# A fused attention and softplus layer on one core: a first product on 256 tokens, full-width transposes and a schedule planned around pieces of the instruction stream

## The chip, the cores and the metric

One core of a Trainium2 chip. The time is the device time of one execution in microseconds (us), and the median of several runs is quoted. Each experiment was timed in the same rounds as the kernel before, on the same chip, because chips differ: the kernel before had medians of 201.96 us in the first job and 198.81, 199.34, 199.85 and 199.41 us in the four later ones. So ratios are compared, not medians of different jobs. The profile comes from one extra execution of each kernel, and the span it covers is some 2 us shorter than the time.

## The reference, cut to what matters

```python
q, k, v, f_logit: (4, 8, 768, 48)          # batch, heads, tokens, head width
f = sigmoid(f_logit)
for t in range(768):                        # a gated running state for each head
    state = f[t][:, None] * state + outer(k[t], v[t])
    y[t] = q[t] @ state
x = y rearranged to (3072, 384)             # tokens, heads * width
out = softplus(x @ w_in) @ w_out            # w_in 384 x 2048, w_out 2048 x 384
```

The kernels cut the 3072 tokens into 24 blocks of 128. A block's attention is a chain of small matmuls; then come the "first product" (x @ w_in), the softplus, and the "second product" (@ w_out). TensorE does all matmuls. In these kernels every result goes to PSUM, which the program lays out as eight banks of 512 floats a partition, and ScalarE or VectorE reads ("evacuates") a bank before the program uses it again.

## The kernel before

The order of all instructions comes from a list scheduler that runs while the kernel is built. Each task has an engine, an estimated duration, what it depends on, and the PSUM banks that it takes (`acq`) and gives back (`rel`).

```python
    ps = [psum.tile([128, 512], FP32, name=f"ps{i}") for i in range(8)]   # one tile, one bank
    def bank(key):
        return ps[P.bank[key]]
    ...                                             # 32 small transposes a block
    def t_T(n):
        for x in range(2):
            for p in range(4):
                for u in range(2):
                    for g in range(2):
                        mm(o[g*64:g*64+64, c:c+64], a[u*64:u*64+64, x*8+g*4+p, :], ident[...],
                           is_transpose=True, tile_position=(u*64, g*64))
    ...
    def t_M(n, g):                                  # one evacuation for each bank
        ... in0=bank(("PU", n, g))[:, 0:256] ...
    def t_F1(n, b):                                 # 128 tokens: 12 matmuls of 128 columns to a bank
        for i in range(4):
            for j in range(3):
                mm(o[:, i*128:i*128+128], w_in[j][:, f*128:f*128+128], xT[n % NX][:, j, :], ...)
    ...                                             # transfers: 4 blocks, w_in, w_out, the rest
    for t in P.run():
        t.fn()
```

## Time and profile before

| | kernel before |
|---|---|
| time, first job | 201.96 us (199.61 to 203.14) |
| span in the profile | 198.9 us |
| TensorE busy | 174.9 us, 88% |
| VectorE, ScalarE busy | 93.3 us, 109.3 us |
| matmuls | 4184 |
| packets of TensorE's instruction stream | 32 |

The two products in the page's list of groups. The columns after the bar are busy time, mean ns of one, and the engine's idle time just before them with what ended most of it. PE is TensorE, PEld its weight loads, ACT ScalarE, DVE VectorE, POOL GpSimd and SP SyncE; "issue" means that nothing that the profile shows was waited for.

```profile
L187 PE MATMUL ps<-xT,w_in 128*128 128x128 bf16 x1152 | 78.1, 224 | 4.4 <-issue 1.6
...
L187 PE MATMUL ps<-w_out,G 128*128 128x384 bf16 x384 | 72.8, 326 | 0.0
```

### The profile page before, as it was taken

What the parts mean: (1) busy time and instruction counts of PE and PEld (TensorE: products, weight loads), DVE (VectorE), ACT (ScalarE), POOL (GpSimd) and SP (SyncE); (2) the same over time, 40 slices, a digit from 0 to 9 for tenths busy, and PEclk for the clock granted to TensorE, in tenths of its full rate; (3) what the DMA queues carried; (4) which work ended last, traced back from release to release, by engine and by line L of the source; (5) the groups of instructions that cost most, each with busy time, mean ns of one, the idle gap of its engine ahead of it and who ended that gap; (6) DMA issues with size and microseconds to landing.
All of it is one profiled execution on the core that took longest, in us unless ns stands there. A gap on an engine that the chain in (4) does not pass through costs nothing.

```text
span 198.9 us, 9400 instructions
## 1 busy us (share of the span) xinstructions
PE 174.9 (88%) x4184; PEld 136.9 (69%) x4184; DVE 93.3 (47%) x268; ACT 109.3 (55%) x241; POOL 54.9 (28%) x75
## 2 busy tenths in 40 slices
PE   0274689999988896999999989999999999999993
PEld 0153478877566675778777768786877778878861
DVE  4287941011774589364336234662455555551012
ACT  2464134559368675676787627864673455435420
POOL 6003860013562365153524012442244300000000
PEclk9999999999999999999999999999999999999999
DMA  6998999999878698899999898894011101110112
GB/s 127 186 204 159 137 200 205 182 197 186 173 148 170 136 181 194 168 197 199 188 188 214 165 210 191 185 229 152 10 36 43 43 3 43 43 46 3 40 40 79
DMA packets 106408, 27.34 MB, mean 137 GB/s; under 512 B 100480, under 2 KB 105600, under 8 KB 106368
## 3 DMA queue, kind: packets, MB, share of 16 engines
q1 hardware_dynamic: 103296, 23.60, 55.1%
q0 software_dynamic: 3072, 3.15, 10.4%
q8 instruction: 32, 0.52, 1.1%
q14 instruction: 8, 0.07, 0.1%
HBM read 25.17 MB, written 4.72 MB: 150 GB/s over the span
## 4 chain that ended last, share of the span: by engine, by line
PE 81%; SPq 6%; DMA 5%; issue 3%; DVE 2%; POOL 1%; DVEq 0%
PE ps L187 81%; SPq L221 6%; DMA w_in<-in_moe_w_in_dram 3%; DMA qkb<-in_k_dram 2%; POOL w_in L256 1%; DVE osb L442 1%; DVE st L361 1%; DVE xT L418 0%; DVE pm L342 0%; DVE tt L355 0%; DVE qkT L317 0%; DVEq L442 0%; DVEq L317 0%
## 5 line engine op out<-in xcount | busy, mean ns | idle before, releaser
L187 PE MATMUL ps<-xT,w_in 128*128 128x128 bf16 x1152 | 78.1, 224 | 4.4 <-issue 1.6
L432 ACT ACTIVATE G<-ps 128x512 bf16<-128x512 f32 x96 | 57.3, 597 | 40.3 <-PE ps L187 37.6
L187 PEld LDWEIGHTS <-w_in 128*128 128x128 bf16 x1152 | 70.0, 100 | 11.2 <-issue 3.9
L187 PE MATMUL ps<-w_out,G 128*128 128x384 bf16 x384 | 72.8, 326 | 0.0
L295 POOL TENSOR_TENSOR qs<-qkb,et 128x768 bf16<-128x768 f32 x20 | 33.0, 1652 | 72.9 <-issue 26.8
L187 PEld LDWEIGHTS <-G 128*128 128x128 bf16 x384 | 34.1, 98 | 17.3
L442 DVE COPY osb<-ps 128x384 f32<-128x384 f32 x24 | 13.3, 556 | 50.2 <-PE ps L187 48.8
L418 DVE COPY xT<-ps 128x192 bf16<-128x192 bf16 x48 | 10.2, 252 | 33.1 <-PE ps L187 25.2
L402 ACT ACTIVATE ysb<-ps 128x192 bf16<-128x192 f32 x48 | 13.5, 329 | 20.6 <-PE ps L187 19.6
L317 DVE COPY qkT<-ps 128x512 bf16<-128x512 bf16 x48 | 18.1, 416 | 7.5 <-PE ps L187 7.2
L342 DVE TENSOR_TENSOR pm<-ps,mask 128x256 bf16<-128x256 f32 x48 | 18.1, 416 | 4.5 <-PE ps L187 4.5
L282 ACT ACTIVATE et<-ps,bq 128x384 bf16<-128x384 f32 x24 | 13.9, 579 | 10.2 <-PE ps L187 10.1
L361 DVE SCALAR_TENSOR_TENSOR st<-tt,gt 128x192 bf16<-128x192 f32 x40 | 17.7, 442 | 1.0
L187 PEld LDWEIGHTS <-qs 64*64 64x64 bf16 x1120 | 15.0, 115 | 4.1 <-DVE qs L295 2.2
L187 PE MATMUL ps<-zt,negU 128*128 128x384 bf16 x24 | 8.5, 354 | 10.2 <-ACT zt L269 10.2
L269 ACT ACTIVATE zt<-fb 128x384 bf16<-128x384 f32 x24 | 12.6, 523 | 6.9 <-DMA fb<-in_f_logit_dram 6.9
L187 PEld LDWEIGHTS <-qkT 64*64 64x64 bf16 x736 | 11.3, 112 | 5.8 <-issue 2.2
L301 POOL CAST vs<-vb 128x384 bf16<-128x384 f32 x20 | 10.4, 524 | 15.5 <-DMA vb<-in_v_dram 15.3
L355 DVE SCALAR_TENSOR_TENSOR tt<-ps,st 128x192 f32<-128x192 f32 x40 | 14.1, 352 | 0.7
L286 ACT ACTIVATE et<-ps,bk 128x384 bf16<-128x384 f32 x24 | 13.8, 577 | 0.0
L187 PE MATMUL ps<-ident,qs 64*64 64x64 bf16 x768 | 11.4, 201 | 2.6 <-DVE qs L295 1.8
L187 PEld LDWEIGHTS <-zt 128*128 128x128 bf16 x96 | 6.2, 100 | 10.3 <-issue 8.5
(35 smaller groups left out, 88.8 us busy)
## 6 DMA issues: line engine op xcount, KB each, us to landing
fb<-in_f_logit_dram SPq DMA_DIRECT2D x24, 192.0 KB, 4.5
qkb<-in_k_dram SPq DMA_DIRECT2D x24, 192.0 KB, 4.2
qkb<-in_q_dram SPq DMA_DIRECT2D x24, 192.0 KB, 4.5
vb<-in_v_dram SPq DMA_DIRECT2D x24, 192.0 KB, 4.4
out_dram<-osb SPq DMA_DIRECT2D x24, 192.0 KB, 3.1
w_in<-in_moe_w_in_dram POOLq DMA_DIRECT2D x12, 128.0 KB, 5.3
w_out<-in_moe_w_out_dram POOLq DMA_DIRECT2D x4, 384.0 KB, 9.1
```

Of the source, the lines that this page charges most:

```text
L187: return pin(nc.tensor.matmul(out=out, lhsT=lhsT, rhs=rhs, start=start, stop=stop, skip_group_check=True, **kw))
L269: pin(nc.scalar.activation(out=zt[n % NZ].rearrange("t p g d -> t g p d")[:, :, :, 0:48], in_=fb[n % NL].rearrange("t (g p) d -> t g p d", ...
L282: pin(nc.scalar.activation(out=et[n % NE][:, 0], in_=bank(("A", n))[:, 0:384], func=AF.Softplus, bias=bq, scale=1.0))
L286: pin(nc.scalar.activation(out=et[n % NE][:, 1], in_=bank(("A", n))[:, 0:384], func=AF.Softplus, bias=bk, scale=-1.0))
L295: pin(eng.tensor_tensor(out=qs[n % NQS][:, :, 0:48], in0=qkb[n % NL].rearrange("t x h d -> t (x h) d"), in1=et[n % NE].rearrange("t x (h d ...
L317: pin(nc.vector.tensor_copy(out=qkT[n % NQT][:, u].rearrange("d x p t -> d (x p t)"), in_=bank(("TX", n, u)).bitcast(BF16)[:, 0:512]))
L342: pin(nc.vector.tensor_tensor(out=pm[n % NPM][:, g], in0=bank(("PU", n, g))[:, 0:256].rearrange("s (p t) -> s p t", p=4), in1=mask, op=ALU ...
L355: pin(nc.vector.scalar_tensor_tensor(out=tt[m % 2], in0=U, scalar=C_P, in1=st[m % NS], op0=ALU.mult, op1=ALU.add))
L361: pin(nc.vector.scalar_tensor_tensor(out=st[(m + 1) % NS], in0=tt[m % 2], scalar=C_UP, in1=gb, op0=ALU.mult, op1=ALU.mult))
L402: pin(nc.scalar.activation(out=ysb[n % NY][:, u], in_=bank(("Y", n, u))[:, 0:192], func=AF.Copy, bias=0.0, scale=1.0))
L432: pin(nc.scalar.activation(out=G[n % NGF][:, 4 * b:4 * b + 4, :].rearrange("f j t -> f (j t)"), in_=bank(("H", n, b)), func=AF.Softplus, b ...
L442: pin(nc.vector.tensor_copy(out=osb[n % NO], in_=bank(("O", n))[:, 0:DM]))
```

## The change

Its intent: fewer instructions for TensorE, so that the pieces of 16 KB (256 instructions) in which they arrive no longer stall it, and fewer, larger evacuations. The core of the diff:

```diff
+PAGE, PAGE0, FETCH = 256, 63, 4.8          # the scheduler now models the pieces
-    ps = [psum.tile([128, 512], FP32, name=f"ps{i}") for i in range(8)]
+    ps = [psum.tile([128, 2, 512], FP32, name=f"ps{i}") for i in range(4)]
     def bank(key):
-        return ps[P.bank[key]]
+        i = P.bank[key]
+        return ps[i // 2][:, i % 2]
+    def two(key):                           # both banks of a tile, for a joined evacuation
+        return ps[P.bank[key + (0,)] // 2]
     def t_T(n):                             # 8 transposes of 128 x 128 for 32 of 64 x 64
+                mm(o[:, i:i + 128], qs[n % NQS][:, x, p].rearrange("t g d -> t (g d)"), ident,
+                   is_transpose=True)
-    def t_M(n, g):                          # likewise the outputs (t_ye) and their transposes (t_xe)
+    def t_M(n):
+            ... in0=two(("P", n))[:, :, 0:256] ...
     def t_F1(n, b):                         # n now counts pairs of blocks
-                mm(o[:, i * 128:i * 128 + 128], ..., xT[n % NX][:, j, :], ...)
+                mm(bank(("H", n, b))[:, i * 256:i * 256 + 256], ..., xT[n % NX][:, j] (256 columns))
+    ORD = [2, 0, 4]                         # transfers: 2 blocks, w_in, 4 blocks, w_out, the rest
...                                          # cut: new scheduler rules, split of t_qs, buffer counts
```

## The prediction

> **What bounds the kernel now.** I read the page from the top, then the chain of waits, then the timeline of TensorE in two stretches. The page first:
>
> ```profile
> span 198.9 us, 9400 instructions
> PE 174.9 (88%) x4184; PEld 136.9 (69%) x4184; DVE 93.3 (47%) x268; ACT 109.3 (55%) x241; POOL 54.9 (28%) x75
> ...
> PE   0274689999988896999999989999999999999993
> ...
> q8 instruction: 32, 0.52, 1.1%
> ...
> PE 81%; SPq 6%; DMA 5%; issue 3%; DVE 2%; POOL 1%; DVEq 0%
> ```
>
> TensorE is the only engine near full, and it carries 81% of the chain that ended last. Its slices (5 us each) fill only from about 25 us; there are dips in slices 12 to 16 (55 to 80 us), then it is solid. VectorE (47%) and ScalarE (55%) have room. The queue of instructions brought 32 packets of 16 KB; 2 x 4184 records in 32 packets are 261 an instruction packet, so nearly all of these are TensorE's own stream. The chain in order of time says what the holes are:
>
> ```profile
> 13.59 4.21 DMA qkb<-in_k_dram
> ...
> 20.15 5.24 DMA w_in<-in_moe_w_in_dram
> 25.39 0.14 issue
> 25.52 2.88 PE ps L187 x34
> ...
> 63.27 0.78 issue
> ...
> 68.10 0.77 issue
> ...
> 76.89 1.64 issue
> ...
> 132.33 45.13 PE ps L187 x1145
> 177.51 17.98 PE ps L187 x232
> 195.56 0.56 DVE osb L442
> ```
>
> Two different things are seen. Up to 25.5 us the chain is transfers: w_in is queued behind the keys of block 3. Later there are pieces called "issue", where TensorE waits for no semaphore. I counted TensorE's records (loads and matmuls together, 63 taken as already passed at the start, as the new model assumes): the stalls before 64.05, 68.87, 78.53, 82.80 and 132.33 us all stand at the first record of a new group of 256, so they are waits for the instruction stream itself. Two neighbouring ones begin 4.82 us apart (64.05 and 68.87). Idle time of PE there: 0.78 + 0.77 + 1.64 + 0.16 = 3.35 us up to 83 us, and about 0.3 at 132, so some 4 us with the pipeline's refilling.
>
> Where TensorE is solid, the timeline prices each kind of work by the distance of starts (a row's own length holds the pipeline's latency too):
>
> ```profile
> 141.79 1.46 PE L187 MATMUL ps<-w_out,G 128*128 128x384 bf16 x8
> 143.18 0.31 PE L187 MATMUL ps<-vs,pm 64*64 64x48 bf16 x16
> 143.33 0.42 PE L187 MATMUL ps<-ident,qs 64*64 64x64 bf16 x32
> 143.58 0.30 PE L187 MATMUL ps<-qkT 64*64 64x64 bf16 x16
> 143.71 0.30 PE L187 MATMUL ps<-vs,qs 64*64 64x48 bf16 x16
> 143.84 0.33 PE L187 MATMUL ps<-st,qkT 64*64 64x48 bf16 x16
> 143.99 0.29 PE L187 MATMUL ps<-ident,ysb 64*64 64x64 bf16 x12
> 144.21 0.82 PE L187 MATMUL ps<-w_out,G 128*128 128x384 bf16 x4
> 144.93 1.51 PE L187 MATMUL ps<-xT,w_in 128*128 128x128 bf16 x24
> 146.28 0.33 PE L187 MATMUL ps<-zt,negU 128*128 128x384 bf16 x1
> 146.44 0.24 PE L187 MATMUL ps<-negsel,zt 128*128 128x2 bf16 x4
> 146.55 1.50 PE L187 MATMUL ps<-xT,w_in 128*128 128x128 bf16 x24
> ```
>
> First product: 24 matmuls from 144.93 to 146.28, 56 ns each. Second product: 0.82 us for 4 of which one lasts 0.326 (the page's mean), so (0.82 - 0.326) / 3 = 163 ns. Cumulative sums: 0.27 us. The merged section of a block's attention: 143.18 to 144.21, 1.03 us, of which the 32 small transposes are 0.25 (143.33 to 143.58); before it, 8 second-product matmuls took 1.39 us instead of 1.30, so entering the section costs 0.09 more. A block of 128 tokens: 48 x 0.056 = 2.70, 16 x 0.163 = 2.61, 0.27 and 1.12: 6.70 us. Times 24 blocks: 161 us. TensorE ends at 195.6, so about 35 us are lost: by 25.5 us about 21 (it has done the attention of less than four blocks, 4 to 5 us of work); then some 5 more up to 35 us, where first-product matmuls lie 106 ns apart ((2.51 - 0.29) / 21 in the stretch from 25.52); about 4 to the instruction stream; the last 5 to sections that are not merged before block 8 and short waits.
>
> **What the Trainium skill says.** "TensorE: Matmul & The Clock Gate", section "Back-to-back issue gap", gives N / 2.4 + 2.5 ns warm: 56, 109 and 162.5 ns at 128, 256 and 384 columns. The trace agrees at both widths that it has (56 and 163). Its Part 1 gives half the clock after idling, 107 ns at 128 columns; the trace has 106 before 35 us. Its Part 4, on transposes, measures about 275 ns for a full-width one in a kernel; the trace has only small ones, and I take the distance, not the duration, as for other matmuls. "Runtime: NRT & Kernel Launch", section "Instruction fetch mechanics", says that instructions come in 16 KiB blocks of 256 and that the crossing is "mostly hidden". The size agrees (261 records a packet); "mostly" does not hold between 60 and 83 us, where four crossings cost 3.35 us.
>
> **The change part by part.**
> 1. First product on 256 tokens: 1152 matmuls at 56 ns (64.5 us) become 576 at 109 (62.8): -1.7 us, and 1152 instructions fewer with the weight loads. Weight loads hide already (PEld 69%).
> 2. Full-width transposes: 768 small ones (24 x 0.25 = 6.0 us) become 192 of 128 columns: 8 x 56 = 0.45 a block, 10.8 us. That is +4.8 us of TensorE, with another 1152 instructions fewer. Parts 1 and 2 alone add 3 us: a block costs 6.83, all blocks 164 us.
> 3. Instructions: 4184 matmuls become 3032, so 2 x 3032 / 261 = 23 packets in place of 32. A block falls from 349 records to 253; at 6.8 us a block a packet is used up in 6.9 us, where it was 4.9, almost the 4.82 at which the crossings stalled. I expect 3 to 4 of the 4 us back.
> 4. Merged evacuations. A copy of 192 columns takes 252 ns and one of 512 takes 416: 0.51 ns a column and 153 fixed. Joining pairs saves about 0.15 x 3 kinds x 24 = 11 us of VectorE, and 24 x 0.17 = 4 us of ScalarE. Neither is on the path where TensorE is solid; it shortens the chains of the first blocks by perhaps 0.5 us each.
> 5. Order of transfers: two blocks, all of w_in, four blocks, w_out, the rest; before: four blocks, w_in, w_out, the rest. w_in can start when the queries of block 1 are in (about 11 us) rather than at 18.1, so its first half is there by 18 to 19 in place of 25.4. The first product starts at 20 when block 1's chain is through, not at 25.5. But blocks 2 to 5 then start at about 21, take 4.1 us each (16 issues took the sync queue to 17 us), and w_out is whole only at 46, where the second product began before 40. TensorE has gaps between 28 and 41 us in exchange. Work done by 46, by the prices above: attention of 5.5 blocks at 1.59 = 8.7, two pairs of first product 10.5, most of a pair of second 4.7: 24, so 22 us lost. Before, by 45: 4.5 x 1.39 + 3.5 x 2.70 + 1.6 x 2.61 = 20, so 25 lost. Gain 3 us.
> 6. Merging from block 6 rather than 8, and fewer split sections: perhaps 2 of the last 5 us.
>
> Sum: 164 of work + 22 up to 46 us + 4 later = 190 us for TensorE's end, against 195.6. With the same 3.3 us of last copy and store the span is 193, 5.6 us or 2.8% less. Compared with the median of 202.45 I take 196.
>
> **The rivals.** (a) The head gets worse: the second product waits for w_out and TensorE starves between 28 and 46 us, with the slow clock as well. The page speaks for it (the transfers already move 160 to 200 GB/s in this stretch and cannot be sped up), against it that three pairs of first product need no w_out. It would cost 3 to 6 us: 200 to 203. (b) Banks become the bound: first-product, second-product (two for a pair), transposes, scores and outputs ask for more than eight at times, so TensorE would wait for ScalarE's softplus (597 ns against 655 ns of matmuls a bank). Nothing is seen of that before (85 to 178 us is nearly solid); it would cost 0.1 to 0.3 us a block, 2 to 7 us: 198 to 203. (c) The head gains as much as w_in comes earlier, since TensorE later never catches up: 5 to 7 us rather than 3, and the time is 190 to 192. (d) Full-width transposes do not pipeline at 56 ns: at twice that +11 us, 206. The neighbouring full-width matmuls speak against it.
>
> **Range and chances.** The work (164) is known to 1 or 2 us, the head to about 4, the stalls to 2: together about 5, so 189 to 201 should hold it 8 times in 10. Faster by 2% means below 198.4: 0.72. Slower needs (a) and (b), or (d): 0.06.
>
> **What would show it.** Instruction packets near 23 and no "issue" stalls of 0.5 us or more after 50 us (step 3); first-product starts 109 ns apart (1); eight transposes in 0.45 us (2); w_in's first half by 19 us, first product from 20, w_out whole at 46 (5); PE at 9 tenths from about 45 us on. I am wrong if TensorE is idle for many microseconds after 50 us, or if the head holds more than 25 us of loss by 46.

## More of the kernel before

The scheduler picks numbers 0 to 7 for the banks. The emitted program is then given its semaphores by the framework, which looks at which tile each instruction reads and writes.

## The result, and the profile after

The changed kernel takes 221.69 us (221.32 to 222.44, 4 runs) against 201.96. A ratio here is the mean time of one kernel's fast runs over that of the other's fast runs of the same rounds, so it is not quite the ratio of the medians: 1.1025, with a 95% interval of 1.092 to 1.113. It is 10% slower, where 3% faster was predicted.

The page of the changed kernel, the rows that answer to those of before (PEclk is the clock that was granted to TensorE, in tenths, in 40 slices of 5.5 us):

```profile
span 219.9 us, 7002 instructions
PE 183.7 (84%) x3032; PEld 133.7 (61%) x3032; DVE 87.9 (40%) x199; ACT 105.1 (48%) x217; POOL 60.5 (27%) x101
...
PE   0557745778997999889898899998999989999993
...
PEclk9999975569999999999999999999999999999998
...
q8 instruction: 23, 0.38, 0.7%
...
PE 70%; ACT 14%; DVE 9%; issue 3%; DMA 1%; DVEq 0%; ACTq 0%
```

The instruction packets fell to 23, as counted beforehand. But ScalarE and VectorE have entered the chain that ended last (14% and 9%, where VectorE alone had 2%), although both do less work than before. That is what a wait that goes back and forth between engines would look like, not an engine that is full. TensorE's clock, too, is down in slices 6 to 9.

```profile
L251 PE MATMUL ps<-xT,w_in 128*128 128x256 bf16 x576 | 74.0, 281 | 8.0 <-ACT G L504 5.2
L251 PE MATMUL ps<-w_out,G 128*128 128x384 bf16 x384 | 69.8, 326 | 3.5 <-ACT G L504 1.5
```

TensorE is idle before both products now, and the softplus (G) ended the largest part of it: 5.2 of 8.0 us and 1.5 of 3.5.

**Where the time came from.** To place it, I priced TensorE's work by the distance of starts in solid stretches: 55.8 ns for a first-product matmul of 128 columns, 109 for one of 256, 162.5 for the second product, 56 for a full-width transpose, 8 to 9.5 for the small matmuls, 0.27 us for a block's sums. "Loss" is the time that has passed less the work done by then, read from the profiles' matmul records (us). Matmuls at half the clock count as loss too:

| kernel | work | loss by 45 us | 45 to 85 | 85 to the last matmul | last matmul starts |
|---|---|---|---|---|---|
| before | 154.8 | 26.4 | 9.3 | 4.6 | 195.1 |
| changed | 157.9 | 32.7 | 7.8 | 17.4 | 215.8 |

The end moved by 20.7 us: 3.1 of work, 6.3 in the head, 1.5 back between 45 and 85 us, and 12.8 lost after 85 us, where before TensorE was solid. The last is the largest piece. Two stretches of the changed kernel's timeline show what it consists of:

```profile
105.68 1.08 ACT L504 ACTIVATE G<-ps 128x512 bf16<-128x512 f32 x2 [1.03 <-DVE qkT L389]
106.65 0.58 ACT L355 ACTIVATE et<-ps,bk 128x384 bf16<-128x384 f32 x1
107.84 1.57 ACT L504 ACTIVATE G<-ps 128x512 bf16<-128x512 f32 x3 [0.60 <-PE ps L251]
```

```profile
106.33 2.12 PE L251 MATMUL ps<-xT,w_in 128*128 128x256 bf16 x18 [0.52 <-ACT G L504]
108.97 0.81 PE L251 MATMUL ps<-xT,w_in 128*128 128x256 bf16 x6 [0.52 <-ACT G L504]
```

Six matmuls fill a bank, so the first bank of this run is full at about 107.15 (106.33 + 5 x 0.109 + 0.28 for the last one). ScalarE is idle from 107.23. It starts the softplus only at 107.84, when the second bank has been written too (11 x 0.109 + 0.28 after 106.33 is 107.81). Then TensorE stops, until 108.97, for a softplus.

```profile
176.48 4.47 PE L251 MATMUL ps<-xT,w_in 128*128 128x256 bf16 x36 [0.53 <-DVE osb L514]
177.33 1.25 ACT L504 ACTIVATE G<-ps 128x512 bf16<-128x512 f32 x2 [0.75 <-PE ps L251]
178.83 1.25 ACT L504 ACTIVATE G<-ps 128x512 bf16<-128x512 f32 x2 [0.25 <-PE ps L251]
180.33 1.25 ACT L504 ACTIVATE G<-ps 128x512 bf16<-128x512 f32 x2 [0.25 <-PE ps L251]
```

Here 36 matmuls and six softpluses go in a rhythm of 1.50 us for two banks, where the matmuls alone need 12 x 0.109 = 1.31 us. Four banks in two tiles are in use (so the built program says), but the rhythm is that of two buffers.

**Theory A.** The framework orders accesses by tile. With a tile of two banks, a softplus of one bank waits for the last matmul written to the tile, also when that went to the other bank; and a matmul waits for the last reader of the tile, also of the other bank. I checked this in the semaphore waits of the built programs:

| waits in the built program | before | changed |
|---|---|---|
| evacuations that wait for matmuls later than the last of their own data | 0 | 81 |
| TensorE waits for a reader of the same tile's other bank | 0 | 93 |
| TensorE waits for a reader of its own bank | 202 | 24 |

In the first stretch above, the softplus of group 4 waits, by the program, for the last matmul of group 5, in the other bank of the same tile; and group 7 waits for the softplus of group 5 although its own bank was read by that of group 4.

**Theory B**, the rival: eight banks are too few for pairs of blocks of 128 tokens, or softplus comes in bursts, whatever the tiles. **Theory C**: the joined evacuations hold two banks too long. **Theory D**, for the head: the new order of transfers.

The kernel's own scheduler, which treats all eight banks as separate, ends its plan at 192.4 us for the kernel before and at 195.7 for the changed one. The spans were 198.9 and 219.9. So it is not the plan that is 20 us longer, it is the distance from the plan.

### The profile page after: what moved, and what is told of

Its sections match the earlier page's. It is cut to its first block, busy times and chain, and to the rows that moved or that the text cites. A ratio compares the mean times of both kernels' runs of the same rounds, so it can differ in the third digit from the quotient of the medians.

```text
span 219.9 us, 7002 instructions
## 1 busy us (share of the span) xinstructions
PE 183.7 (84%) x3032; PEld 133.7 (61%) x3032; DVE 87.9 (40%) x199; ACT 105.1 (48%) x217; POOL 60.5 (27%) x101
## 4 chain that ended last, share of the span: by engine, by line
PE 70%; ACT 14%; DVE 9%; issue 3%; DMA 1%; DVEq 0%; ACTq 0%
PE ps L251 70%; ACT G L504 7%; DVE qkT L389 4%; ACT et L355 4%; DVE osb L514 2%; DMA fb<-in_f_logit_dram 1%; DVE tt L439 1%; DVE pm L425 1%; ACT zt L343 1%; ACT gt L359 1%; ACT L343 1%; ACT ysb L479 0%; DVE st L444 0%; DVE qs L364 0%; DVE xT L493 0%
## 5 line engine op out<-in xcount | busy, mean ns | idle before, releaser
L251 PE MATMUL ps<-xT,w_in 128*128 128x256 bf16 x576 | 74.0, 281 | 8.0 <-ACT G L504 5.2
L251 PEld LDWEIGHTS <-w_in 128*128 128x128 bf16 x576 | 57.1, 100 | 20.8 <-issue 11.1
L364 POOL TENSOR_TENSOR qs<-qkb,et 128x384 bf16<-128x384 f32 x42 | 37.8, 916 | 75.4 <-ACT et L355 72.0
L493 DVE COPY xT<-ps 128x384 bf16<-128x384 bf16 x24 | 8.5, 356 | 51.5 <-PE ps L251 27.1
L479 ACT ACTIVATE ysb<-ps 128x384 bf16<-128x384 f32 x24 | 11.8, 490 | 26.5 <-PE ps L251 25.2
L389 DVE COPY qkT<-ps 128x1024 bf16<-128x1024 bf16 x24 | 16.6, 690 | 18.0 <-PE ps L251 12.4
L251 PEld LDWEIGHTS <-qs 64*64 64x64 bf16 (+1 forms) x544 | 19.3, 114 | 6.4 <-POOL qs L364 2.1
L251 PE MATMUL ps<-ident,qs 128*128 128x128 bf16 x192 | 16.8, 238 | 4.6 <-ACT zt L343 2.0
L425 DVE TENSOR_TENSOR pm<-ps,mask 128x512 bf16<-128x512 f32 x24 | 16.3, 681 | 0.0
L251 PEld LDWEIGHTS <-qkT 64*64 64x64 bf16 x736 | 11.2, 114 | 8.1 <-DVE qkT L389 5.3
L251 PE MATMUL ps<-qkT 64*64 64x64 bf16 x384 | 8.0, 205 | 4.9 <-DVE qkT L389 4.0
```

The source lines that it names most:

```text
L251: return pin(nc.tensor.matmul(out=out, lhsT=lhsT, rhs=rhs, start=start, stop=stop, skip_group_check=True, **kw))
L364: pin(eng.tensor_tensor(out=qs[n % NQS][:, x].rearrange("t p g d -> t g p d")[:, :, :, 0:48], in0=qkb[n % NL][:, x].rearrange("t (g p) d - ...
L389: pin(nc.vector.tensor_copy(out=qkT[n % NQT].rearrange("d x p t -> d (x p t)"), in_=bank(("T", n)).bitcast(BF16)))
L425: pin(nc.vector.tensor_tensor(out=pm[n % NPM].rearrange("s g p t -> s g (p t)"), in0=two(("P", n))[:, :, 0:256], in1=mask.rearrange("s g p ...
L479: pin(nc.scalar.activation(out=ysb[n % NY], in_=two(("Y", n))[:, :, 0:192], func=AF.Copy, bias=0.0, scale=1.0))
```

## The experiments

Twelve kernels ran; all were correct. "Evac. split" means that the three joined evacuations are written as two instructions, one for each bank:

```diff
-            out=pm[n % NPM]..., in0=two(("P", n))[:, :, 0:256], in1=mask...
+        for g in range(2):
+            out=pm[n % NPM][:, g]..., in0=bank(("P", n, g))[:, 0:256], in1=mask[:, g]...
```

**1. One-bank tiles** (evac. split; the order of tasks is the same plan):

```diff
-    ps = [psum.tile([128, 2, 512], FP32, name=f"ps{i}") for i in range(4)]
+    ps = [psum.tile([128, 512], FP32, name=f"ps{i}") for i in range(8)]
-        return ps[i // 2][:, i % 2]
+        return ps[i]
```

> The changed kernel with eight one-bank PSUM tiles in place of four two-bank ones; the three joined evacuations are split in two, the order of all instructions stays. Theory A (a tile of two banks is one object to the dependency tracker, so 81 evacuations wait for later matmuls in the other bank and 93 TensorE waits are for a reader of the other bank): the 12 to 13 us that TensorE loses after 85 us go, 207 to 211 us, and the waits of the first product for softplus nearly vanish. Rival B (too few banks for pairs of tokens, or softplus in bursts, whatever the tiles): 219 to 224 us, since the plan and its banks are the same and the evacuations only got dearer.

Measured: 203.48 us, ratio to before 1.0209 (1.013 to 1.028). Of the 10.25% that the change lost, 8.2% came back, some 16 us, although the evacuations had to be split. Run 2 below has the same split and was timed in the same rounds: against it, one-bank tiles alone are worth 20.0 us (the mean of the fast runs is 203.0 against 223.0). The built program has none of the 81 and 93 false waits. The span is 201.2 us against the same plan of 195.7: the distance fell from 24.2 to 5.5 us. It went a little beyond what A expected, because the false waits had cost time before 85 us as well: the loss by 45 us fell from 32.7 to 29.7, and that from 45 to 85 us from 7.8 to 2.9. The groups and the timeline of this kernel:

```profile
L250 PE MATMUL ps<-xT,w_in 128*128 128x256 bf16 x576 | 71.4, 280 | 0.7 <-DVE xT L493 0.5
...
L250 PE MATMUL ps<-w_out,G 128*128 128x384 bf16 x384 | 69.4, 326 | 0.0
```

```profile
159.45 4.75 PE L250 MATMUL ps<-xT,w_in 128*128 128x256 bf16 x42
...
160.30 4.53 ACT L506 ACTIVATE G<-ps 128x512 bf16<-128x512 f32 x7 [0.71 <-PE ps L250]
```

Seven groups, each a bank, are written and read without a gap: 42 matmuls in 4.75 us, 41 x 0.109 + 0.28. The wait for the softplus is gone from the first product.

**2. The control: evacuations split, two-bank tiles kept.**

> The control to the run with one-bank tiles: only the three joined evacuations are split, the tiles keep two banks each. Theory A: no gain, 221 to 225 us (72 more small evacuations, 10 us more of VectorE and 4 of ScalarE, false waits unchanged at 83 and 104). If the joined evacuations themselves held the banks too long (rival C), this run gains several us, to 215 or less.

Measured: 223.08 us, ratio 1.1228 (1.115 to 1.131). No gain; theory C falls, and the gain of run 1 belongs to the tiles.

**3. The reverse: the kernel before on two-bank tiles**, nothing else changed:

```diff
-    ps = [psum.tile([128, 512], FP32, name=f"ps{i}") for i in range(8)]
+    ps = [psum.tile([128, 2, 512], FP32, name=f"ps{i}") for i in range(4)]
-        return ps[P.bank[key]]
+        i = P.bank[key]
+        return ps[i // 2][:, i % 2]
```

> The kernel before with its eight one-bank tiles laid as halves of four two-bank tiles, nothing else. Theory A: it gets 95 evacuations that wait for later matmuls and 160 waits for a reader of the other bank, so it should lose 5 to 14 us: 207 to 216 us. Rival B: nothing changes, 200 to 204 us.

Measured: 219.10 us, ratio 1.1032 (1.095 to 1.112): these lines alone make the old kernel as slow as the changed one. The direction was A's, the size above what I gave it (5 to 14 us). Theory B falls as the main cause: neither the pairs of blocks nor the joined evacuations are in this kernel. The granted clock, another possible cause, falls too: its mean was 0.999 in this slow kernel, and 0.962 in run 1, close to the 0.958 of the changed kernel.

**4. The changed kernel with the transfers in the order of before** (`ORD = [4, 0, 0]`), two-bank tiles.

> The changed kernel with the transfers in the order of before (four blocks, w_in, w_out, the rest), the schedule planned anew for it. If the new order and its slow-clock gap between 31 and 48 us cost the head about 8 us: 212 to 216 us. If the head is bound by the chain of the first blocks in any order: 219 to 223 us.

Measured: 219.47 us, ratio 1.1011 (1.092 to 1.110), not distinguishable from 1.1025. In its trace the loss by 45 us is 25.4 in place of 32.7, but 11.1 (for 7.8) follow by 85 us and 18.9 (for 17.4) after it. Nearly 5 of the 7 us won in the head are given back while the false waits rule.

**5. One-bank tiles and the order of before** (runs 1 and 4 together).

> One-bank tiles and the transfers in the order of before. If the order of transfers costs the head some 3 to 4 us (TensorE's loss by 45 us is 29.7 us with the new order on one-bank tiles, 26.4 in the kernel before): 199 to 201 us, 2.5 to 4 us under the run with one-bank tiles alone and level with the kernel before or a little better. If the order does not matter: 203 to 204.

Measured: 200.39 us, ratio 1.0164 (1.006 to 1.027). The intervals of this and run 1 overlap. The traces say 3 us: loss by 45 us 24.7 against 29.7, last matmul at 194.2 against 197.2. So the order of transfers costs about 3 us by the traces; these two timings, from different jobs, don't separate it. In this job only three of the seven runs of the kernel before count as fast (196.03 to 198.71), so the ratios of runs 5 to 8 are on the high side, and they are better compared with each other.

**6. One-bank tiles, small transposes inside the sections** (`TT = 0`, order of transfers as changed).

> One-bank tiles, the changed kernel's order of transfers, and transposes of 64 by 64 merged in the sections as before (48 records a block more in the instruction stream). If full-width transposes cost 4.6 us of TensorE and save less than that in stalls of the instruction stream: 199 to 202 us. If the 16 KB pieces decide (the plan's own model says 202.4 of span against 195.7): 206 to 211 us, with several us of issue stalls at the boundaries of 256 records.

Measured: 208.03 us, ratio 1.0535 (1.042 to 1.065), 3% slower than run 1 with its full-width transposes by the ratios, and 2% slower than run 7 of the same job (which also lacks the term for pieces). My reading, that they cost TensorE 4.6 us for nothing, was wrong. The work did fall to 153.3 us, but the loss rose from 39.3 to 48.5. In its trace the one wait at a boundary of 256 instructions that stands out left TensorE idle for 0.19 us, so it is not the stalls themselves.

**7. One-bank tiles, no term for pieces in the scheduler** (`FETCH = 0.0`).

> One-bank tiles, the term for 16 KB pieces taken out of the schedule model (their time set to 0). With 253 records a block there are no stalls to plan around, so nothing: within 1 percent of the run with one-bank tiles, 202 to 205 us. If the model's term had been earning its keep: 206 us or more, with issue stalls.

Measured: 203.72 us, ratio 1.0322 (1.022 to 1.042), against 1.0209; the intervals just overlap. One stall at a boundary, of 0.55 us, appears. With so few instructions the term does nothing that these runs can show.

**8. One-bank tiles, order of before, small transposes.**

> One-bank tiles, order of transfers of before, small transposes: what stays of the change is the first product on 256 tokens, the split of the scaled keys and queries in two, and the schedule model. If the costs of full-width transposes (4.6 us) and of the order (3 us) add up: 195 to 198 us, 1 to 2 percent under the kernel before. If stalls of the instruction stream come back: 200 to 205.

Measured: 203.88 us, ratio 1.0337 (1.024 to 1.044). Two stalls at boundaries, of 0.66 and 2.20 us, are back. The costs that I had hoped to add up do not. But runs 5 to 8 share a job, and two pairs of them differ in one setting. Run 8 is run 6 with the old order of transfers: its fast runs have a mean of 203.99 us against 207.89, and no run of one reaches into the other's range. So here the timings do show the cost of the new order, 3.9 us. And run 8 is run 5 with small transposes: 203.99 against 200.57, so these cost 3.4 us.

**9. Two tiles of two banks for the pairs only, four tiles of one bank for all else**, joined evacuations kept:

```diff
-    ps = [psum.tile([128, 2, 512], ...) for i in range(4)]
+    ps = [psum.tile([128, 2, 512], ...) for i in range(2)]
+    one = [psum.tile([128, 512], ...) for i in range(4)]
     # the scheduler takes pairs from banks 0 to 3 and single banks from 4 to 7
```

> The changed kernel with two tiles of two banks that only the pairs use (scores and outputs, so the joined evacuations stay) and four tiles of one bank for all else; order of transfers unchanged. Theory A: the first product, the sums, the transposes and the second product have banks of their own again, so most of the 18 us come back without splitting any evacuation: 203 to 208 us. If one-bank tiles had won by the splitting or by the freer choice of banks: 212 us or more.

Measured: 203.94 us, ratio 1.0192 (1.012 to 1.027), the same as run 1. The false waits are down to 7 and 12. So it is the sharing of a tile by unrelated results that costs, not the joined reading of two banks that belong together.

**10. Run 5 with TensorE warmed up**: 24 groups of four matmuls of constants in idle time, starting after the transposes of block 2, read by nobody.

> One-bank tiles, order of transfers of before, and 24 groups of four matmuls of constants, whose result nobody reads, in TensorE's idle time between about 16 and 26 us, so that its clock is up when the first product starts. If the slow clock until 33 us costs the head its 107 against 56 ns: TensorE's loss at 35 us falls from 24.8 to 21 us and the time to 196 to 198 us, 1 to 2 percent under the kernel before. If the head is bound by transfers and the chain of the blocks: 200 to 202 us.

Measured: 200.27 us, ratio 1.0045 (0.996 to 1.014); run 5 had 200.39 and 1.0164 in another job. The clock did come up, from 19.6 us on (33.1 in run 5), but at 29.9 it fell again for 3.4 us, after the first product had waited for its weights:

```profile
26.02 0.27 PE L250 MATMUL ps<-xT,w_in 128*128 128x256 bf16 x1 [0.22 <-DMA w_in<-in_moe_w_in_dram]
27.33 0.27 PE L250 MATMUL ps<-xT,w_in 128*128 128x256 bf16 x1 [1.04 <-DMA w_in<-in_moe_w_in_dram]
28.57 0.60 PE L250 MATMUL ps<-xT,w_in 128*128 128x256 bf16 x4 [0.96 <-DMA w_in<-in_moe_w_in_dram]
```

The loss at 35 us is 24.8 with and without the warming. A miss for the first half of my expectation: up to there this head waits for its transfers, and the earlier clock gains nothing. A head that stays at full clock throughout was not tried.

**11. Run 9 with the order of before.**

> Two two-bank tiles for the pairs, four one-bank tiles, joined evacuations kept, transfers in the order of before. If what the tiles and the order cost simply add up (18 us and 3 us off 221.7): 199 to 202 us, level with the kernel before within 1.5 percent, and none of the joined evacuations had to be given up.

Measured: 201.29 us, ratio 1.0049 (0.997 to 1.013). As expected: level with the kernel before.

**12. Run 6 without the term for pieces.**

> One-bank tiles, small transposes in the sections, and no term for 16 KB pieces in the schedule model. The small transposes lost 5 us to the full-width ones though they take 4.6 us less of TensorE. If the plan's caution about pieces was what cost them: 200 to 204 us (the plan without it is 3.5 us shorter), with perhaps 2 us of real stalls. If the longer sections themselves cost it (a section waits for more): 206 to 210 us as with the term.

Measured: 207.18 us, ratio 1.0395 (1.033 to 1.046); the loss is 46.9 us. The ratio is not apart from that of run 7, the same kernel with full-width transposes (1.0322, 1.022 to 1.042), but in the traces the last matmul starts at 200.2 us against 197.1. So the caution of the scheduler explains at most a part. Two things narrow down the rest. The plan itself is longer: with small transposes it ends at 202.4 us, without the term for pieces at 198.9, where run 1 has 195.7. And in runs 6, 8 and 12 the clock falls to half once more in the middle, for 3.4 us from 79.2, 6.8 from 57.6 and 3.4 from 79.3, which no kernel with full-width transposes does between 50 us and its last matmul. That a section with the transposes in it must wait for more at once would fit both; it is argued and not shown.

The losses as defined above, with the total at the last matmul (us):

| kernel | work | loss by 45 us | 45 to 85 | after 85 | total | ratio to before |
|---|---|---|---|---|---|---|
| before | 154.8 | 26.4 | 9.3 | 4.6 | 40.4 | 1 |
| changed | 157.9 | 32.7 | 7.8 | 17.4 | 57.9 | 1.1025 |
| run 1, one-bank tiles | 157.9 | 29.7 | 2.9 | 6.7 | 39.3 | 1.0209 |
| run 3, before on two-bank tiles | 154.8 | 28.2 | 11.2 | 21.0 | 60.5 | 1.1032 |
| run 5, one-bank tiles, old order | 157.9 | 24.7 | 5.6 | 6.0 | 36.4 | 1.0164 |
| run 6, one-bank tiles, small transposes | 153.3 | 29.9 | 8.2 | 10.4 | 48.5 | 1.0535 |

Run 3 loses 16.4 us more after 85 us than the kernel before, run 1 loses 10.7 less than the changed one: the two-bank tiles take it away and give it back in both kernels. No version is clearly faster than the kernel before. The best, runs 10 and 11, are level with it.

## Why the prediction was wrong, point by point

**The step that failed.** In the sum "164 of work + 22 up to 46 us + 4 later" the work held (157.9 us by the prices above, without the cost of entering sections). What failed most is the "4 later": TensorE lost 25.2 us after 45 us, and 9.6 in run 1, where only the tiles and the split are different. The "22" failed too: 32.7 by 45 us, of which one-bank tiles give back 3.0 (see step 5). Both signs that the prediction named for being wrong came. Rival (b) was the nearest to it: it was sized at "0.1 to 0.3 us a block, 2 to 7 us", on the ground that "Nothing is seen of that before (85 to 178 us is nearly solid)". It looked at how many banks are wanted, not at what the program waits for; and in run 1 the same eight banks, under the same plan, were enough. The diff had the line that matters, four tiles of two banks for eight of one. In the sum I counted it only through part 4, the joined evacuations, as a saving off the path. What the runs showed in its place: that line costs 20.0 us in the changed kernel (run 1 against run 2) and 10.3% in the old one (run 3). The case against (b) was drawn from the kernel before, in which the cause did not exist.

**Steps 1 to 3 held.** First-product matmuls lie 109 ns apart (42 in 4.75 us). Eight full-width transposes take 0.46 us in the changed kernel:

```profile
144.24 0.62 PE L251 MATMUL ps<-ident,qs 128*128 128x128 bf16 x8
144.70 0.81 PE L251 MATMUL ps<-w_out,G 128*128 128x384 bf16 x4
```

The packets are 23 and no stall stands at a boundary of 256. That the stalls before came in steps of 256 records can be counted: 1116, 1244, 1500, 1628 and 2780 matmuls, each with its load, go before them, and the differences are multiples of 128. On one-bank tiles the loss between 45 and 85 us fell from 9.3 to 2.9 us (5.6 with the old order of transfers). The 3 to 4 us that I gave the instruction stream fit into that, but were not measured apart. Rival (d) fell. Two sums are a little off: (0.82 - 0.326) / 3 is 165, not 163 (the matmuls of the second product do start 162 to 163 ns apart), and 202.45 less 5.6 is 197, not 196. The formula N / 2.4 + 2.5 that the prediction takes from the Trainium skill ("TensorE: Matmul & The Clock Gate", section "Back-to-back issue gap") is given there for an isolated matmul; here it held for pairs of weight load and matmul too, with 56 ns at 128 columns and 109 at 256. But to book the transposes as a net cost of 4.8 us was wrong in the other direction: runs 6 and 8 without them are slower.

**Step 5 had the wrong sign.** The first product does start early, at 18.73 us (20 was predicted), but at the slow clock: 24 matmuls in 5.27 us, 0.213 us apart where 0.109 is usual (the clock's records, and PEclk with them, begin to say something only at 23.9 us).

```profile
18.73 5.27 PE L251 MATMUL ps<-xT,w_in 128*128 128x256 bf16 x24 [0.46 <-DVE xT L493]
```

After it, the clock is at half from 30.7 to 47.7 us by the clock's records, and w_out comes late, for a reason I had not looked at. GpSimd issues it, in order, after a product that waits for ScalarE:

```profile
44.09 0.91 POOL L364 TENSOR_TENSOR qs<-qkb,et 128x384 bf16<-128x384 f32 x1 [3.55 <-ACT et L355]
44.94 3.06 POOL L310 DMA_DIRECT2D w_out<-in_moe_w_out_dram  x4
```

The transfers that it was to follow had been issued by 36.2 us, and I had counted all of it as landed at 46. Loss by 45 us: 32.7, where I had 22 by 46. On one-bank tiles it is 29.7, with the order of before 24.7. How much of this is the slow clock and how much the late w_out was not separated. So a gain of 3 us became a cost: 5 us at that point, 3 us at the end of the trace (runs 1 and 5), and 3.9 us in the timed runs 6 and 8, with small transposes. This was rival (a), the head, at its stated size.

**Step 4** was right that the evacuations themselves are off the path: run 9, with them, equals run 1, without. Of the 11 us of VectorE that they were to save, its busy time shows 5.4 (93.3 to 87.9). **Step 6** was not tested on its own.

**What stays open:** the last 0 to 2% between the changed kernel on separate banks and the kernel before, which is near the noise of these runs, and why small transposes in the sections lose more time than they save.

## What to carry to other kernels

When a change regroups a buffer, look at what unit the dependencies are tracked in: two results that share a tile share its waits, even if each lies in a bank of its own. A plan that counts eight free banks is only as good as the waits the program is given, so compare the plan with the trace; a chain of waits that alternates between engines none of which is full was the sign here. And when a rival is weighed against the old profile, ask whether what could cause it exists there at all.

## What the Trainium skill lacked or had wrong

- "PSUM — Partial Sum Buffer", section "PSUM bank collisions raise a hardware error", advises to guard PSUM by bank and quadrant. In these runs waits by bank were enough: the results were correct, and 20.0 us came back (run 1 against run 2). Whether anything coarser or finer would raise the error was not tried. No page says what a tile of several banks does to the waits, which here cost 10.3% in a kernel changed in nothing else (run 3, 219.10 us).
- "Runtime: NRT & Kernel Launch", section "Instruction fetch mechanics", calls the crossing of a 16 KiB block "mostly hidden". In the kernel before, crossings between 63 and 83 us left TensorE idle for 0.78, 0.77, 1.64 and 0.16 us; with 253 instead of 349 records a block of tokens none did in the changed kernel, and one in run 5 (0.77 us) and in run 7 (0.55). The page gives no rate at which it stops being hidden; two stalled crossings here were 4.82 us apart.
- "TensorE: Matmul & The Clock Gate", Part 4, gives about 275 ns for a full-width transpose in a kernel. As a duration that is near what the page of the changed kernel has (238 ns mean); in a row they start 55 to 56 ns apart (8 in 0.46 us with the change to the next kind of work), which the page does not say and which is what a plan needs.
